# Half of the stored queries keep their centred products, and their features are made when attention takes them

## The chip, the cores and the metric

The kernel runs on one core of one Trainium2 chip. The metric is the device time of one execution in microseconds (us), here the median of several runs. All arithmetic is float32, and products are made from operands that are split into a high and a low part.

## The reference

The input `x` has 2048 rows of 512 columns. Every row is normalised, and the normalised rows go through two branches, whose results are multiplied.

```
xn  = layernorm(x)
q, k, v = split(xn @ wqkv)              # 32 heads of 16
phi(t) = where(t > 0, t + 1, exp(t)) + 1e-6
kv  = sum over rows of phi(k) v ;  z = sum over rows of phi(k)
s   = (phi(q) kv) / (phi(q) z + 1e-6) @ wo
h   = gelu(layernorm(xn) @ w1), its four column groups shifted by +1, -1, +2, -2 rows
x1  = xn + h @ w2
b   = x1 + gelu(layernorm(x1) @ w3) @ w4     # hidden width 1376
out = x + s * silu(b)
```

What matters here is `phi(q)`, the feature of a query. It is needed only after `kv` and `z` are complete, that is, after all rows have passed once. Since `where(t > 0, t + 1, exp(t))` equals `min(exp(t), 1) + relu(t)`, it also equals `exp(-relu(-t)) + relu(t)`.

## The kernel before, in words

The rows are worked on in 16 tiles of 128 rows; four tiles make a block (`QT` = 4, `NQ` = 4 blocks). The program has two stages.

In the first stage, up to about 235 us, every block passes through keys and queries, the sums over keys (`gram`) and the mixer (`mixer`, `mix2`, `mixed`). Blocks 0 and 1 make keys and queries by `key` and `query`, one tile at a time. Blocks 2 and 3 make them in `keys_queries` (line 839), a pair of tiles at a time with seven products in place of eight; its tiles `p1`, `p5` and `u2` hold products that are already centred. The key features are made there and then by `feature_k`: on ACT (ScalarE) a Relu into `kr` and an Exp into `kt`, then on DVE (VectorE) a scalar_tensor_tensor of the two. The query features are made by `feature_q` (line 802): on ACT a Relu of the negated product into `e`, a Relu into `r`, and an Exp of `e`; then `r` is stored in memory as `pqd` by SP's queue, and `e` is added to it there by a DMA that POOL (GpSimd) issues with accumulation (`gather`, line 220). In the profile these are the names `qe` and `qr`, and the transfers `pqd<-qr` and `pqd<-qe`. `by_chunk` and `by_block` are views that reorder the columns on the way.

In the second stage the four blocks go one after the other through the large products (`up_pair`, `down`), attention and the gate. Within a block, `turn_q` (line 1168) is called for two tiles when group 2 of the columns is worked on and for the other two at group 3. It fetches the stored features (`pq<-pqd`) and divides them by their denominators on DVE: a scalar_tensor_tensor into `qz`, a reduction into `den`, a reciprocal into `rd`, another scalar_tensor_tensor; then it turns them by way of memory. `forms_q` and `attend_pair` take what it leaves. ACT in this stage evicts the products (`p`, `u`, `p1s` and so on), makes the Gelus (`gf`, `f_..`) and the Tanhs of the gate (`th`). Exp and Gelu need different function tables on ACT; Relu, Copy and Identity run with either.

After each block's mixer, `mixed` (line 988) makes the second normalisation: statistics on DVE, then on POOL `w`, `rs` (a power) and `nm`, then on ACT the four tiles `y`, which DVE turns and SP stores.

The order of every engine's instructions is not the order of the calls. `Plan.emit` takes the operations as a graph, gives each a due time that is worked out back from a nominal sequence on TensorE, and lays them out one by one on the engines with estimated durations; among those ready it takes the one that is due first. So a change of one operation can reorder all the later ones on every engine. `SOONER` is a table of pairs, an operation's number in the graph and a number of quarter microseconds by which it is due earlier. Tiles named `p` come from 96 pieces of memory in SBUF, and `mm` and `acc` are the eight banks of PSUM.

Of the kernel before, what the change touches and what calls it, by code (L numbers as in the profile page):

```python
# [10 lines left out]
AF = mybir.ActivationFunctionType  # L11
ALU = mybir.AluOpType
# [384 lines left out]
def linear_attn_gated_by_mixer(  # L397
# [20 lines left out]
    QT = 4  # L418
# [7 lines left out]
    PIECE = BT + W  # L426
    EARLY = (), ()
    SUMS = "DVE"
    SOON = {"T": 30.0, "u": 5.0}
    AHEAD = 70.0, 50.0, 30.0, 10.0, 0.0  # L430
    TH = BT // 2
# [11 lines left out]
    pl = Plan(nc, pools, counts, ("acc", "mm"))  # L443

    def piece(name, dt=F32):
        return pl.new("p", name, dt, PIECE)[:, :512]

    def rounds(name):

        return piece(name + "h", F32R), piece(name + "l", F32R)  # L450

    def memory(name, width=512, rows=P):
        return pl.new("dram", name, F32, width, rows)
# [4 lines left out]
    def fixed(name, n, dt=F32):  # L458

        t = pl.new("const", name, dt, n)  # L460
        t.ap = const.tile([P, n], dt, name=name)
        return t
# [38 lines left out]
    rs1, rs2, ns1, nm1, nm2, au = (fixed(n, NT) for n in ("rs1", "rs2", "ns1", "nm1", "nm2", "au"))  # L501
# [31 lines left out]
    def col(t, i):  # L533
        return t[:, i:i + 1]
# [55 lines left out]
    def small(name, n):  # L590
        return pl.new("sm", name, F32, n)
# [80 lines left out]
    def make_u(b):  # L672
# [12 lines left out]
        for n, u, v, op in ((0, q[1, 0], q[1, 1], ALU.add), (1, parts[0], q[0, 0], ALU.subtract),  # L685
                            (2, q[0, 0], q[1, 0], ALU.subtract), (3, q[0, 1], parts[1], ALU.subtract)):
            for c in range(2):
                pl.tt(parts[n][c], u[c], v[c], op, eng=SUMS)
            hl = rounds(f"us{b}_{n}")
# [36 lines left out]
    def by_chunk(v):  # L726

        return v.via(lambda ap: ap.rearrange("p (c b k) -> p c b k", b=P // RB, k=RB))

    def by_block(v):  # L730

        return v.via(lambda ap: ap.rearrange("p (b c k) -> p c b k", b=P // RB, k=RB))
# [67 lines left out]
    pqd = {i: memory(f"pqd{i}") for i in range(NT)}  # L800

    def feature_q(i, t):
        e, r = (piece(f"q{n}{i}") for n in "er")
        pl.act(by_block(e), by_chunk(t), AF.Relu, scale=col(ns1, i))
        pl.act(by_block(r), by_chunk(t), AF.Relu, scale=col(rs1, i))
        pl.act(e, e, AF.Exp, scale=-1.0)
        pl.soon(pl.store(pqd[i].all, r))
        pl.soon(pl.gather(pqd[i].all, e))

    def query(i):  # L810
        ps = bank(f"q{i}")
        project(ps, i, WQ, range(NC))
        t = piece(f"qt{i}")
        pl.stt(t, qneg, mean(mv1, i), ps, ALU.mult, ALU.add)
        feature_q(i, t)
# [23 lines left out]
    def keys_queries(b, j):  # L839

        i, k = b * QT + j, b * QT + j + 2
        pa, pb, pe = (bank(f"{n}k{i}") for n in ("pa", "pb", "pe"))
        p1, p5, u2 = (piece(f"{n}k{i}") for n in ("p1", "p5", "u2"))

        def go(ps, x, y, start=True):
            products(ps, [both(U[b][x][c], j * P, (j + 1) * P) + TW[y][c] for c in range(2)], start, more=not start)

        go(pb, "a11", "b11")
        pl.act(p1, pb, AF.Copy)
        go(pe, "s1", "t1")  # L850
        pl.act(p5, pe, AF.Copy)
        go(pb, "s2", "t2", False)
        pl.act(u2, pb, AF.Copy)
        go(pa, "a12", "b21")
        pl.tt(p1, pa, p1, ALU.add)
        go(pb, "s3", "t3", False)
        pl.tt(p5, pb, p5, ALU.add)
        go(pe, "s4", "b22", False)
        pl.tt(u2, u2, pe, ALU.add)
        feature_k(i, p1, True)  # L860
        go(pb, "a22", "t4", False)
        feature_k(k, pb, True)
        feature_q(i, u2)
        feature_q(k, p5)
# [303 lines left out]
    def turn_q(i):  # L1168

        pq, t = piece(f"pq{i}"), piece(f"qz{i}")  # L1170
        pl.fetch(pq, pqd[i].all)
        pl.stt(t, pq, TINY, zb, ALU.add, ALU.mult)
        den, rd = small(f"den{i}", H).all, small(f"rd{i}", H).all
        pl.add("DVE", .6, .68, [t], [den], lambda: nc.vector.tensor_reduce(
            den.get(), t.get().rearrange("p (h d) -> p h d", d=DH), axis=AX.X, op=ALU.add))
        pl.ts(den, den, DEN_EPS, None, ALU.add)
        pl.add("DVE", .28, .35, [den], [rd], lambda: nc.vector.reciprocal(rd.get(), den.get()))
        v = pq.via(lambda ap: ap.rearrange("p (h d) -> p h d", d=DH))
        pl.stt(v, v, TINY, rd.via(lambda ap: ap[:, :, None].to_broadcast([P, H, DH])), ALU.add, ALU.mult)
        turned = Turned(f"q{i}", 1)  # L1180
        turned.put(0, pq)
        turned.take()
        QTT[i] = turned
# [208 lines left out]
    for what, *args in ORD:  # L1392
        pl.early = SOON.get(what, 0.0)
        DO[what](*args)
# [11 lines left out]
    for base, s in ((0, 1), (DH - 1, -1)):  # L1406
        v = bmask.all.via(lambda ap: ap.rearrange("p (h d) -> p h d", d=DH))
# [35 lines left out]
    for b in range(NQ):  # L1443
# [5 lines left out]
        for n, fs in enumerate(groups):  # L1449
# [14 lines left out]
            if n > 0:  # L1464
                for k in range(2):
                    if n == (2, 3)[k]:
                        for j in range(2):
                            turn_q(b * QT + 2 * k + j)
                        forms_q(b * QT + 2 * k)
                    if n == (4, 5)[k]:  # L1470
                        pairs.append(b * QT + 2 * k)
# [18 lines left out]
        else:  # L1490
# [3 lines left out]
            t = piece(f"xi{i}", F32R)  # L1494
# [13 lines left out]
                gate(b * QT + QT - 1, a, o, D // 2, late=True, by_dma=False, whole=o > 0)  # L1508

    SOONER = (  # L1510
        36, 64, 186, 8, 199, 16, 1412, -8, 1489, 8, 1493, 41, 1549, 16, 1982, 4, 2419, -8, 2854, 16, 3165, 8,
        4113, -8, 4394, -8, 4725, 64, 4805, 16, 4810, 65, 4814, -32,
    )
    pl.emit(first=6.0, lead={"p": 14.0, "w": 14.0, "ab": 10.0}, reserve={"p": 20, "w": 1, "ab": 0}, window=12.0,
            ahead=6.0, table=SOONER)
# [37 lines left out]
```

## Time and profile before

| | |
|---|---|
| median of 3 runs | 517.55 us |
| lowest and highest | 516.91 and 520.1 us |
| the profiled execution | 517.69 us, of it a span of 515.8 us from the first to the last instruction |
| granted TensorE clock | 0.999 |
| instructions in the span | 8950 |

The profile is of one execution. Its engines are PE (TensorE's products), PEld (its weight loads), DVE, ACT, POOL and SP. A row of a timeline gives the start and the duration in us, then the engine, the line, the operation, the tile written and the tiles read, the shape and the count, and in brackets the idle time of the engine before it with what ended it. Most rows name the line of a helper (L147 for products, L168 for ACT, L190, L195 and L200 for DVE and POOL, L224 for the DMAs that POOL issues), so the names of the tiles tell what is what. The end of a product is modelled: a product of 512 columns is shown with about 0.4 us, while the next one starts 0.23 us after it.

### The profile page before, as it was taken

What the parts mean: (1) busy time and instruction counts of PE and PEld (TensorE: products, weight loads), DVE (VectorE), ACT (ScalarE), POOL (GpSimd) and SP (SyncE); (2) the same over time, 40 slices, a digit from 0 to 9 for tenths busy, and PEclk for the clock granted to TensorE, in tenths of its full rate; (3) what the DMA queues carried; (4) which work ended last, traced back from release to release, by engine and by line L of the source; (5) the groups of instructions that cost most, each with busy time, mean ns of one, the idle gap of its engine ahead of it and who ended that gap; (6) DMA issues with size and microseconds to landing.
All of it is one profiled execution on the core that took longest, in us unless ns stands there. A gap on an engine that the chain in (4) does not pass through costs nothing.

```text
span 515.8 us, 8950 instructions
## 1 busy us (share of the span) xinstructions
PE 507.6 (98%) x2983; PEld 441.1 (86%) x2983; DVE 412.4 (80%) x832; ACT 337.9 (66%) x694; POOL 104.6 (20%) x191
## 2 busy tenths in 40 slices
PE   9999999999999999999999999999999999999996
PEld 7677788898778878898899989899898898999985
DVE  5987669999879996989999998655796659965545
ACT  5899778775979989878767644355443455643521
POOL 1589311244521732211100011000020000110000
PEclk9999999999999999999999999999999999999999
DMA  8978961989695999999875859577486594499404
GB/s 274 318 206 153 287 153 36 263 254 247 218 267 155 244 318 249 281 183 334 286 212 155 281 174 254 180 191 209 132 212 227 179 233 156 114 278 303 119 5 120
DMA packets 78194, 109.05 MB, mean 211 GB/s; under 512 B 8396, under 2 KB 31460, under 8 KB 78148
## 3 DMA queue, kind: packets, MB, share of 16 engines
q1 hardware_dynamic: 68788, 91.44, 55.5%
q0 software_dynamic: 9360, 17.04, 19.8%
q8 instruction: 23, 0.38, 0.3%
q14 instruction: 23, 0.19, 0.1%
HBM read 67.15 MB, written 32.91 MB: 194 GB/s over the span
## 4 chain that ended last, share of the span: by engine, by line
PE 77%; ACT 14%; DVE 3%; DMA 2%; issue 2%; POOL 1%; SPq 0%; ACTq 0%; DVEq 0%; POOLq 0%
PE acc L147 23%; PE pb L147 11%; PE pe L147 6%; PE pbs L147 4%; PE h L147 4%; PE g L147 4%; PE k L147 3%; PE pbm L147 3%; PE pa L147 3%; PE pes L147 2%; PE a L147 2%; ACT qe L168 2%; PE pbk L147 2%; PE q L147 2%; DMA o<-x 2%
## 5 line engine op out<-in xcount | busy, mean ns | idle before, releaser
L224 POOL DMA_DIRECT2D th<-in_x x14 | 12.4, 939 | 245.8 <-DVE th L200 108.5
L224 POOL DMA_DIRECT2D o<-x x16 | 14.6, 975 | 59.7 <-DVE o L190 47.3
L168 ACT ACTIVATE p<-pb 128x256 f32<-128x256 f32 x20 | 7.6, 382 | 27.3 <-PE pb L147 27.1
L190 DVE TENSOR_TENSOR gf<-pa,p 128x256 f32<-128x256 f32 x20 | 8.4, 418 | 18.8 <-PE pa L147 15.3
L168 ACT ACTIVATE th<-xo 128x512 f32<-128x512 f32 (+1 forms) x16 | 9.8, 620 | 20.0 <-DVE xo L190 19.9
L224 POOL DMA_DIRECT2D zacc<-kr x16 | 15.2, 949 | 36.8 <-DVE kr L200 22.7
L168 ACT ACTIVATE gf<-gf 128x512 f32<-128x512 f32 (+1 forms) x40 | 20.8, 523 | 0.8
L168 ACT ACTIVATE p<-pe 128x256 f32<-128x256 f32 x20 | 7.7, 384 | 17.5 <-PE pe L147 17.5
L224 POOL DMA_DIRECT2D pqd<-qe x16 | 14.8, 927 | 20.4 <-DMA pqd<-qr 8.8
L190 DVE TENSOR_TENSOR xo<-acc,xo 128x512 f32<-128x512 f32 (+1 forms) x16 | 10.4, 670 | 10.6 <-PE acc L147 9.6
L190 DVE TENSOR_TENSOR gf<-u,pe 128x256 f32<-128x256 f32 x20 | 8.3, 417 | 9.9 <-PE pe L147 9.8
L168 ACT ACTIVATE y<-o,nm,rs 128x512 f32<-128x512 f32 x16 | 12.1, 803 | 3.4 <-POOL nm L195 3.4
L168 ACT ACTIVATE ht<-ht 128x512 f32<-128x512 f32 x16 | 9.7, 626 | 6.5 <-DVE ht L190 6.4
L200 DVE SCALAR_TENSOR_TENSOR kr<-kt,kr 128x512 f32<-128x512 f32 x16 | 10.9, 683 | 3.7 <-ACT kt L168 3.6
L190 DVE TENSOR_TENSOR ht<-h,abc 128x512 f32<-128x512 f32 x16 | 10.7, 680 | 3.4 <-PE h L147 3.4
L168 ACT ACTIVATE x<-x,nm,rs 128x512 f32<-128x512 f32 x16 | 12.8, 810 | 0.0
L168 ACT ACTIVATE u<-pb 128x256 f32<-128x256 f32 x20 | 7.7, 384 | 6.0 <-PE pb L147 6.0
L200 DVE SCALAR_TENSOR_TENSOR th<-th,so 128x512 f32<-128x512 f32 (+1 forms) x17 | 10.9, 653 | 0.5
L200 DVE SCALAR_TENSOR_TENSOR pq<-pq,rd 128x512 f32<-128x512 f32 x16 | 11.0, 687 | 0.2
L601 POOL TENSOR_TENSOR rs<-w,nhalf 128x4 f32<-128x4 f32 (+2 forms) x10 | 10.7, 1074 | 0.7
L200 DVE SCALAR_TENSOR_TENSOR qz<-pq,zb 128x512 f32<-128x512 f32 x16 | 10.7, 685 | 0.2 <-DMA pq<-pqd 0.2
L168 ACT ACT_TABLE_LOAD x8 | 10.3, 1283 | 0.9 <-PEq L1544 0.8
(1682 smaller groups left out, 2239.1 us busy)
## 6 DMA issues: line engine op xcount, KB each, us to landing
w_s<-in_w SPq DMA_DIRECT2D x28, 256.0 KB, 4.7
x<-in_x SPq DMA_DIRECT2D x16, 256.0 KB, 3.5
zacc<-kr POOLq DMA_DIRECT2D x16, 256.0 KB, 5.1
pqd<-qr SPq DMA_DIRECT2D x16, 256.0 KB, 3.2
pqd<-qe POOLq DMA_DIRECT2D x16, 256.0 KB, 6.7
o<-x POOLq DMA_DIRECT2D x16, 256.0 KB, 6.3
x1d<-o SPq DMA_DIRECT2D x16, 256.0 KB, 5.7
pq<-pqd SPq DMA_DIRECT2D x16, 256.0 KB, 3.5
```

The source lines that it names most:

```text
L147: lambda: nc.tensor.matmul(out.get(), lhs.get(), rhs.get(), start=start, stop=stop, skip_group_check=more))
L168: nc.scalar.activation(out.get(), src.get(), func, scale=get(scale), **kw)
L190: self.vec(eng, out, [a, b], lambda: self.e(eng).tensor_tensor(out.get(), a.get(), b.get(), op=op), True)
L200: lambda: self.nc.vector.scalar_tensor_tensor(out.get(), a.get(), get(s), b.get(), op0=op0, op1=op1),
L224: lambda: self.nc.gpsimd.dma_start(out.get(), get(src), accum_op=ALU.add), mb=mb)
L601: lambda: g.tensor_tensor(out.get(), src.get(), nh.get(), op=ALU.pow))
```

## The change

For the tiles of the last two blocks (numbers 8 to 15), `feature_q` only stores the centred product. `turn_q` fetches it and makes the feature there, as keys have it: Relu, Exp, and min and sum in one scalar_tensor_tensor. The tiles of blocks 0 and 1 stay as they are. The table `SOONER` is another one: it has 13 pairs in place of 17. The graph has eight operations less.

```diff
+    LATE = 2 * QT
...
     def feature_q(i, t):
+        if i >= LATE:
+            pl.soon(pl.store(pqd[i].all, t))
+            return
         e, r = (piece(f"q{n}{i}") for n in "er")
         pl.act(by_block(e), by_chunk(t), AF.Relu, scale=col(ns1, i))
         pl.act(by_block(r), by_chunk(t), AF.Relu, scale=col(rs1, i))
         pl.act(e, e, AF.Exp, scale=-1.0)
...
     def turn_q(i):
         pq, t = piece(f"pq{i}"), piece(f"qz{i}")
-        pl.fetch(pq, pqd[i].all)
+        if i < LATE:
+            pl.fetch(pq, pqd[i].all)
+        else:
+            v, r = piece(f"qv{i}"), piece(f"qr{i}")
+            pl.fetch(v, pqd[i].all)
+            pl.act(by_block(r), by_chunk(v), AF.Relu, scale=col(rs1, i))
+            pl.act(by_block(pq), by_chunk(v), AF.Exp, scale=col(rs1, i))
+            pl.stt(pq, pq, 1.0, r, ALU.min, ALU.add)
         pl.stt(t, pq, TINY, zb, ALU.add, ALU.mult)
...
     SOONER = (
-        36, 64, 186, 8, 199, 16, 1412, -8, 1489, 8, 1493, 41, 1549, 16, 1982, 4, 2419, -8, 2854, 16, 3165, 8,
-        4113, -8, 4394, -8, 4725, 64, 4805, 16, 4810, 65, 4814, -32,
+        50, 32, 186, 2, 666, 16, 711, 8, 780, 4, 1431, 16, 2110, 16, 2323, 16, 3582, 16, 4095, 32, 4672, 32,
+        4788, 32, 4797, 16,
     )
```

## The prediction

> **What bounds the kernel now.** I read the page's parts 1 and 2 first, then busy time by stretches, then the timelines of the engines around each hole of PE.
>
> ```profile
> span 515.8 us, 8950 instructions
> PE 507.6 (98%) x2983; PEld 441.1 (86%) x2983; DVE 412.4 (80%) x832; ACT 337.9 (66%) x694; POOL 104.6 (20%) x191
> ```
>
> PE is busy for all but 8.2 us of the span. The number of products does not change, so a gain can only come out of those 8.2 us, while a loss can be of any size. Where they lie is seen in the stretches (columns: stretch, its length, then busy time and count of PE, PEld, DVE, ACT, POOL; granted clock; DMA share; GB/s):
>
> ```profile
> 0.00:20.00 20.00, 18.70 (x70) 13.94 (x71) 14.21 (x29) 12.90 (x26) 4.58 (x19) 1.00 0.89 314
> 20.00:60.00 40.00, 39.30 (x169) 30.42 (x168) 32.05 (x64) 37.90 (x69) 30.40 (x66) 1.00 0.88 208
> 60.00:120.00 60.00, 60.00 (x339) 52.01 (x338) 52.83 (x105) 45.02 (x86) 16.38 (x26) 1.00 0.74 192
> 120.00:220.00 100.00, 98.65 (x476) 80.41 (x474) 87.22 (x182) 86.78 (x157) 35.36 (x60) 1.00 0.92 246
> 140.00:160.00 20.00, 19.03 (x85) 14.73 (x84) 15.62 (x32) 16.57 (x31) 4.62 (x7) 1.00 0.84 236
> 220.00:240.00 20.00, 19.88 (x147) 17.64 (x146) 18.41 (x38) 14.61 (x37) 3.45 (x4) 1.00 0.98 241
> 240.00:500.00 260.00, 260.00 (x1728) 237.04 (x1727) 199.69 (x404) 138.63 (x319) 12.67 (x16) 1.00 0.68 200
> 360.00:480.00 120.00, 120.00 (x791) 109.19 (x790) 88.04 (x174) 58.25 (x134) 7.05 (x8) 1.00 0.69 201
> 500.00:520.00 20.00, 11.03 (x67) 9.61 (x65) 8.01 (x15) 2.07 (x4) 1.75 (x2) 0.92 0.30 79
> ```
>
> The idle time of PE is 1.30 us in the first 20, 0.70 at 20 to 60, nothing at 60 to 120, 1.35 at 120 to 220 (0.97 of it in the 20 us from 140 on), 0.12 at 220 to 240, nothing at 240 to 500, and 15.8 - 11.03 = 4.77 at the end; that adds up to 8.24. So the second stage, where the new work goes, has no hole today, and the first stage between 20 and 240 us, which loses work, has 2.17 us, nearly half of it at 140 to 160. That is the place to look at.
>
> ```profile
> 147.14 0.39 PE L147 MATMUL g<-k10h,x10l 128*128 128x512 f32 x1
> 148.01 0.50 PE L147 MATMUL pbk<-wk_0h,u_0h 128*128 128x512 f32 x1 [0.47 <-DVE ht L190]
> 148.34 0.39 PE L147 MATMUL pbk<-wk_0l,u_0h 128*128 128x512 f32 x1
> 148.57 0.40 PE L147 MATMUL pbk<-wk_0h,u_0l 128*128 128x512 f32 x1
> ...
> 150.66 0.40 PE L147 MATMUL pek<-kq_1h,us_0l 128*128 128x512 f32 x1
> 151.47 0.50 PE L147 MATMUL pbk<-kq_0h,us_1h 128*128 128x512 f32 x1 [0.41 <-ACT p1k L168]
> ...
> 154.84 0.40 PE L147 MATMUL pek<-wq_2h,us_3l 128*128 128x512 f32 x1
> 155.32 0.50 PE L147 MATMUL pbk<-kq_0h,us_2h 128*128 128x512 f32 x1
> ```
>
> A product's end is modelled, so I go by starts. From 148.34 to 148.57 the step is 0.23 us. The steps 147.14 to 148.01, 150.66 to 151.47 and 154.84 to 155.32 are 0.87, 0.81 and 0.48, so the holes are 0.64 + 0.58 + 0.25 = 1.47 us. The first waits for DVE, the second for ACT. What made them late stands some microseconds earlier:
>
> ```profile
> 138.84 0.36 DVE L596 BATCH_NORM_AGGREGATE mv<-st 128x2 f32<-128x6 f32 x4
> 140.47 0.94 POOL L224 DMA_DIRECT2D pqd<-qe  x1 [2.89 <-ACT qe L168]
> 141.48 0.33 POOL L195 TENSOR_SCALAR w<-mv 128x4 f32<-128x4 f32 x1
> 144.13 0.24 POOL L195 TENSOR_SCALAR nm<-nm 128x4 f32<-128x4 f32 x1
> 144.41 2.93 ACT L168 ACTIVATE y<-o,nm,rs 128x512 f32<-128x512 f32 x4 [3.40 <-POOL nm L195]
> 145.25 1.42 DVE L156 STREAM_TRANSPOSE y_0z<-y 128x512 f32<-128x512 f32 x2 [3.53 <-ACT y L168]
> 147.30 1.25 DVE L190 TENSOR_TENSOR ht<-h,abc 128x512 f32<-128x512 f32 x2
> 147.36 1.28 ACT L168 ACT_TABLE_LOAD   x1
> 150.85 0.57 ACT L168 ACTIVATE p1k<-pbk 128x512 f32<-128x512 f32 x1
> ```
>
> POOL works in order. Its accumulating transfer for a query waited 2.89 us for the Exp of `qe`, and behind it stood the second normalisation of block 1 (`w` to `nm`), whose statistics `mv` were there at 139.2. So ACT stood idle for 3.40 us before the four `y` and DVE for 3.53 before their transposes; then both had everything at once. DVE came to `ht` at 147.30, and PE's bank was freed late; ACT did the four `y`, a table load and Gelus before it evicted `p1k` at 150.85.
>
> **The change part by part.** The prices of the removed and the moved work:
>
> ```profile
> L168 ACT ACTIVATE qe<-qe x16: 613/619/642, 37.5 to 204.2; 128x512 f32<-128x512 f32 x16
> L168 ACT ACTIVATE qe<-p5k,ns x4: 710/722/729, 138.0 to 202.4; 128x512 f32<-128x512 f32 x4
> L224 POOL DMA_DIRECT2D pqd<-qe x16: 853/878/1218, 38.4 to 209.5; - x16
> L200 DVE SCALAR_TENSOR_TENSOR kr<-kt,kr x16: 657/684/693, 21.9 to 199.5; 128x512 f32<-128x512 f32 x16
> L168 ACT ACTIVATE kt<-p1k,rs x4: 709/717/724, 130.5 to 195.2; 128x512 f32<-128x512 f32 x4
> L168 ACT ACT_TABLE_LOAD x8 | 10.3, 1283 | 0.9 <-PEq L1544 0.8
> ```
>
> *Removed, eight times, at 128 to 210 us:* on ACT two Relus of 0.72 (that into `qr` has the shape of that into `qe`) and an Exp of 0.62, 2.06 us, together 16.5; on POOL one issue of 0.88, together 7.0; in memory one accumulating transfer of 256 KB, together 2.1 MB. ACT and DVE are the crowded engines there, yet what counts is PE's holes alone. With no query transfer in POOL's order, `w` can start when `mv` is there, at 139.2 in place of 141.48: 2.3 us earlier, as are the `y`, their transposes, the table load and the Gelus behind them. The three holes are 0.64 us and less, so 2.3 us closes all: **1.47 us**. The bounds are 0 (the new order has a wait of the same size in another place, since ACT, DVE and the key's own transfers stay crowded) and, for all idle time at 20 to 240 us, 2.17 plus the 1.47 - 0.97 = 0.50 that the modelled ends hide: 2.7. I take 1.47, for it is the only part whose cause the change removes.
>
> *The store* stays one issue of SP for a tile; it waits for DVE's product and no longer for a Relu of ACT, so it is not later. No table load goes away there: the keys' Exps stay, and with them the switches.
>
> *Added, eight times, at some 370 to 470 us:* on ACT a Relu and an Exp like those of the keys, 0.72 + 0.72, together 11.5; on DVE one more scalar_tensor_tensor of 0.68, together 5.5. Of both engines there is enough (ACT 58 and DVE 88 of 120 at 360 to 480). The Exps now stand among Gelus and Tanhs, so each pair of tiles costs a table load before and one behind: eight more, 10.3 us more of ACT. Over the span that makes ACT 337.9 - 16.5 + 11.5 + 10.3 = 343.2, DVE 412.4 + 5.5 = 417.9, POOL 104.6 - 7.0 = 97.6.
>
> Here is the risk. ACT works in order, and what stands behind a pair's Exps are the evictions (`p`, `u`, `f`) that PE's next products wait for. With the loads a pair holds ACT for 1.28 + 0.72 + 0.72 + 1.28 = 4.0 us at one piece.
>
> ```profile
> 371.25 1.27 ACT L168 ACTIVATE th<-xo 128x512 f32<-128x512 f32 x2 [4.00 <-DVE xo L190]
> 394.51 0.38 ACT L168 ACTIVATE p<-pb 128x256 f32<-128x256 f32 x1 [4.45 <-PE pb L147]
> ```
>
> ACT has free stretches of 4.00 and 4.45 us just ahead of and in block 2, so a pair fits, barely; and the order can put products into `acc`, which need no eviction, in front of an eviction that is late. Bounds: 0 for all four pairs, and 4 x 4.0 = 16 us if nothing covers them. I take 0, the nearer row being the free stretch of 4.45 us.
>
> The added Relu is also a new wait of ACT for a DMA. It is short of time only once:
>
> ```profile
> 386.82 0.87 SPq L218 DMA_DIRECT2D pq<-pqd  x2
> 390.70 1.29 DVE L200 SCALAR_TENSOR_TENSOR qz<-pq,zb 128x512 f32<-128x512 f32 x2
> ```
>
> There the fetches are issued 3.9 us before DVE uses them. With Relu, Exp and the new step in between the fetch must go about 3 us earlier on SP's queue, or `qz` comes 3 us later; the column group that uses the result is two groups on. I take 0; the bound is one tile's 1.4 us of ACT and 0.7 of DVE, once.
>
> *The table `SOONER`.* It moves due times also ahead of 120 us, where the work is the same. Its price shows in no row; the idle time of 0.70 us at 20 to 60 could go or double, so it lies within 0.7 us either way, and I take 0.
>
> [...] The rows of a load and of what follows show what a switch takes here:
>
> ```profile
> 205.84 1.28 ACT L168 ACT_TABLE_LOAD   x1
> 207.14 1.15 ACT L168 ACTIVATE ht<-ht 128x512 f32<-128x512 f32 x2
> ```
>
> The load takes 1.28 us, and the next instruction starts 0.02 us behind it. [...]
>
> *Sum.* The profiled execution took 517.69 us, 1.89 more than its span, and the median of the runs is 517.55, so the two are alike. 517.69 - 1.47 + 0 + 0 = **516.2 us**.
>
> **The rivals.**
>
> *The stall moves.* For it: ACT and DVE are busy 87 of 100 us at 120 to 220 by the stretches, the key's accumulating transfers stay in POOL's order, and every later instruction is laid out anew. Against it: the chain above runs through one query transfer. Then the time is that of before within the 0.7 us of the table, 517.7 (517.0 to 518.4). The same comes out if the removed transfers were hidden anyway.
>
> *Slower: Exps in the way of evictions.* Place: ACT at 370 to 470 us. Each pair that is not covered costs up to 4.0 us; it decides as soon as 1.5 us are uncovered. One pair uncovered and the gain gone: 517.7 + 4.0 = 521.7; all four, 533. For it: PE has no spare time there and a pair fits only just. Against it: ACT is idle for more than half of that stage. Chiefly I expect one pair: about 520 with the gain, 521.7 without.
>
> *A switch costs twice its row.* Then a pair holds ACT for 6.6 us, 2.1 over the longest free stretch above; four pairs make 8.4, and the time is 516.2 + 8.4 = 524.6. Against it stand the 0.02 us behind the load.
>
> *More than expected.* To come out over 1% lower (5.2 us, about what a measurement of this kernel can tell from no change) the 2.7 us of idle time at 20 to 240 would all have to go, the 1.3 at the start, and 1.2 of the tail's 4.77, which no part of the change touches but the table.
>
> **How the numbers follow.** Forecast 0.45, stall moves 0.33, Exps in the way 0.17, switch twice its row 0.02, more than expected 0.03. The low end is 517.69 less the 2.7 us of idle time, less the 0.6 by which the lowest run lies below the median, 514.3 with rounding. The high end is one uncovered pair without the gain, 521.7. Over 1% slower, above 522.7, needs two uncovered pairs or the dear switch: half of 0.17 and the 0.02, rounded to 0.10; over 1% faster 0.03; the rest 0.87.
>
> **What would show it.** Right: no query transfer in POOL's order; the `y` of block 1 without the wait of 3.4 us before them; no PE hole of 0.5 us or more at 140 to 160; 16 table loads; ACT near 343, DVE near 418, POOL near 98 us; PE at 20.00 in the stretches from 240 to 500. Wrong: PE waits for `p`, `u` or `f` after 360 us; more than 16 loads (the two Exps of a pair apart); the query's fetch as releaser of ACT; or new holes before 240 us as large as the old.

## The result, and the profile after

The changed kernel takes 518.89 us (median of 22 runs, 516.0 to 520.75); the kernel before, run beside it, 517.33 us (22 runs, 516.81 to 520.1). The ratio is 1.0026, interval 1.0013 to 1.0038: slower by 0.26%, some 1.3 us, where 1.47 us less was forecast. Both kernels scatter over 4 us, so each timing below is read with its interval and each reason by traces.

The profiled execution after took 518.31 us. Its totals, from the page's part 1 and one group of part 5:

```profile
span 516.6 us, 8955 instructions
PE 507.4 (98%) x2983; PEld 439.6 (85%) x2983; DVE 418.1 (81%) x840; ACT 343.9 (67%) x692; POOL 100.4 (19%) x183
L168 ACT ACT_TABLE_LOAD x14 | 18.0, 1283 | 3.9 <-PE pb L147 3.0
```

ACT's 343.9 us and DVE's 418.1 came out as counted (343.2 and 417.9). POOL's 100.4 us are 2.8 more than the 97.6 counted, about as much as a single instruction of POOL, `w`, will be seen to last too long. There are 14 table loads and not 16, since the four tiles of block 3 share one pair of loads.

To see where time went, the span is cut at three products: the first of block 0's mixer, the first of the second stage, and the last of all. From PE's timeline, before:

```profile
63.41 0.40 PE L147 MATMUL h<-u_0h,w_0h 128*128 128x512 f32 x1
...
234.44 0.68 PE L147 MATMUL a<-yb110h,w_lh 128*96 128x256 f32 x1
...
510.75 0.28 PE L147 MATMUL accx<-w_9h,f_9l 128*128 128x256 f32 x1
```

and after:

```profile
62.90 0.40 PE L147 MATMUL h<-u_0h,w_0h 128*128 128x512 f32 x1
...
234.57 0.28 PE L147 MATMUL a<-yb110h,w_lh 128*96 128x256 f32 x1
...
511.52 0.28 PE L147 MATMUL accx<-w_9h,f_9l 128*128 128x256 f32 x1
```

The differences of these starts, here and in each experiment's trace (us; "tail" is the rest of the span):

| kernel | span | start | middle | second stage | tail |
|---|---|---|---|---|---|
| before | 515.8 | 63.41 | 171.03 | 276.31 | 5.05 |
| after | 516.6 | 62.90 | 171.67 | 276.95 | 5.08 |
| b_look (before again) | 515.3 | 63.59 | 170.43 | 276.24 | 5.04 |
| a_look (after again) | 517.4 | 63.98 | 171.31 | 276.98 | 5.13 |
| a_again (after again) | 517.9 | 62.91 | 172.94 | 276.95 | 5.10 |
| a_evict_first | 517.4 | 62.82 | 172.49 | 277.02 | 5.07 |
| a_dve_waits | 515.8 | 63.12 | 170.60 | 277.03 | 5.05 |
| a_both | 516.3 | 63.69 | 170.56 | 276.96 | 5.09 |
| a_waits_all | 515.7 | 63.43 | 170.10 | 277.11 | 5.06 |
| b_waits_all | 518.0 | 65.70 | 170.37 | 276.82 | 5.11 |
| b_gather_behind | 515.0 | 63.94 | 169.75 | 276.22 | 5.09 |
| b_table_of_after | 521.7 | 63.37 | 177.08 | 276.22 | 5.03 |
| a_table_of_before | 518.4 | 65.81 | 168.87 | 278.53 | 5.19 |
| a_mixed | 515.3 | 63.45 | 168.65 | 278.03 | 5.17 |
| a_mixed_waits | 516.8 | 64.78 | 168.93 | 277.88 | 5.21 |
| a_exp_twice | 544.1 | 63.31 | 170.02 | 305.70 | 5.07 |
| a_no_loads | 516.7 | 63.38 | 171.66 | 276.63 | 5.03 |

After against before: start -0.5, middle +0.6, second stage +0.6. Some of this is the cut itself. In before the second stage's first product is shown with 0.68 us and the next one starts 0.52 us after it; in after it is 0.28 and 0.12. The 0.40 us between them belong to a product `m` right ahead, which thus counts in the second stage in the one case and in the middle in the other. (With 0.68: before, `b_look`, `b_waits_all`, `b_gather_behind`, `a_table_of_before`, `a_mixed`, `a_mixed_waits`; the others have 0.28.) With `m` counted alike, after's middle is 0.2 us longer than before's and its second stage 1.0. So the middle, which was to get 1.47 us shorter, got no shorter, and the second stage is not free. The start varies by itself: with the old table it is 63.4 to 63.9 us in three traces and 65.7 to 65.8 in two. Such a step of 2.2 us would make the two groups in which the runs of before fall (about 517.3 and 519.7); no run of before itself was traced in the upper one (where the start is lost, the last section says). The median of before lies between 517.3 and 518.8 from one set of runs to another, as fewer or more of its runs fall into that group, so a ratio is compared only with those of its own set.

The stretches of after, with the columns of those of before:

```profile
20.00:60.00 40.00, 39.66 (x171) 30.98 (x170) 32.39 (x65) 37.02 (x67) 28.52 (x66) 1.00 0.90 224
...
120.00:220.00 100.00, 97.48 (x471) 79.83 (x470) 87.86 (x182) 76.14 (x135) 31.40 (x51) 1.00 0.83 228
140.00:160.00 20.00, 20.00 (x103) 16.77 (x101) 17.41 (x35) 18.51 (x34) 2.02 (x4) 1.00 0.77 241
220.00:240.00 20.00, 20.00 (x153) 18.08 (x152) 18.00 (x37) 13.46 (x34) 3.42 (x4) 1.00 0.77 206
240.00:500.00 260.00, 259.75 (x1723) 235.30 (x1722) 203.89 (x408) 155.18 (x341) 13.18 (x16) 1.00 0.68 199
```

The 20 us from 140 on are full (before 19.03), yet the 100 us around them have 2.52 us of idle time (before 1.35). The stall was removed, and a larger one stands elsewhere. The removal, by POOL's and ACT's timelines of after:

```profile
137.52 0.57 POOL L195 TENSOR_SCALAR w<-mv 128x4 f32<-128x4 f32 x1 [0.77 <-DVE mv L597]
...
141.29 2.94 ACT L168 ACTIVATE y<-o,nm,rs 128x512 f32<-128x512 f32 x4 [2.53 <-POOL nm L195]
```

Block 1's `w` now waits for its statistics alone, 0.77 us, and the `y` start 3.1 us earlier (before 144.41), 2.6 counted from the mixer's first product. The new stall is in the same place of the next block, after's second normalisation of block 2 (POOL, then DVE, ACT and PE in the same stretch):

```profile
182.01 0.89 POOL L224 DMA_DIRECT2D zacc<-kr  x1 [7.67 <-DVE kr L200]
182.98 3.17 POOL L195 TENSOR_SCALAR w<-mv 128x4 f32<-128x4 f32 x1
...
182.89 0.69 DVE L200 SCALAR_TENSOR_TENSOR k12l<-kr,k12h 128x512 fp32r<-128x512 f32 x1
183.49 0.69 DVE L190 TENSOR_TENSOR x14l<-x,x14h 128x512 fp32r<-128x512 f32 x1
...
185.37 0.69 DVE L190 TENSOR_TENSOR w_al<-w_s,w_ah 128x512 fp32r<-128x512 f32 x1
185.98 0.69 DVE L200 SCALAR_TENSOR_TENSOR k14l<-kr,k14h 128x512 fp32r<-128x512 f32 x1
...
188.22 1.52 ACT L168 ACTIVATE y<-o,nm,rs 128x512 f32<-128x512 f32 x2 [2.27 <-POOL nm L195]
189.64 0.57 ACT L168 ACTIVATE p1k<-pbk 128x512 f32<-128x512 f32 x1
...
187.76 0.40 PE L147 MATMUL pek<-kq_1h,us_0l 128*128 128x512 f32 x1
190.27 0.50 PE L147 MATMUL pbk<-kq_0h,us_1h 128*128 128x512 f32 x1 [2.11 <-ACT p1k L168]
```

Read it from below. PE steps 2.51 us where 0.23 is usual, a hole of 2.28, because ACT evicts `p1k` behind two `y`, and the `y` come late. POOL's `w` is why: four numbers a row, 0.57 us in block 1, and here 3.17. All that time DVE runs one instruction after another, six of them, and `w` ends at 186.15, right behind the sixth, `w_al` (186.06); the seventh, `k14l`, runs on beside its end. That DVE is the cause is so far an argument.

### The profile page after: what moved, and what is told of

Same layout as the page of the kernel before. It is cut to its first block, busy times and chain, and to the rows that moved or that the text cites. A ratio compares the mean times of both kernels' runs of the same rounds, so it can differ in the third digit from the quotient of the medians.

```text
span 516.6 us, 8955 instructions
## 1 busy us (share of the span) xinstructions
PE 507.4 (98%) x2983; PEld 439.6 (85%) x2983; DVE 418.1 (81%) x840; ACT 343.9 (67%) x692; POOL 100.4 (19%) x183
## 4 chain that ended last, share of the span: by engine, by line
PE 82%; ACT 7%; DVE 5%; DMA 3%; issue 2%; POOL 1%; SPq 1%; DVEq 0%; POOLq 0%
PE acc L147 21%; PE pb L147 10%; PE h L147 9%; PE g L147 5%; PE pe L147 5%; PE pbs L147 4%; PE pbm L147 4%; PE pbk L147 3%; PE pa L147 2%; PE pes L147 2%; PE a L147 2%; PE pem L147 2%; PE k L147 2%; PE q L147 2%; DMA o<-x 1%
## 5 line engine op out<-in xcount | busy, mean ns | idle before, releaser
L596 DVE BATCH_NORM_STATS2 st<-o 128x6 f32<-128x512 f32 x16 | 10.4, 683 | 1.0 <-DMA o<-x 1.0
L190 DVE TENSOR_TENSOR so<-so,xo 128x512 f32<-128x512 f32 (+1 forms) x16 | 10.7, 669 | 0.1
```

The lines of the kernel that those rows point to most:

```text
L190: self.vec(eng, out, [a, b], lambda: self.e(eng).tensor_tensor(out.get(), a.get(), b.get(), op=op), True)
L596: pl.add("DVE", .62, .69, [xv], [st], lambda: nc.vector.bn_stats(st.get(), xv.get()))
```

## The experiments

Labels beginning with a are edits of the kernel after, with b of the kernel before. Diffs are cut to their core; numbers are operations of the graph.

**The new stall.** Three runs ask whether ACT's order or POOL's `w` makes it.

`a_evict_first` lets `p1k` go ahead of the `y`:

```diff
+    hold (y8, y9 and the first transpose of y8) until eviction p1k of tile 13's pair is issued
```

> The kernel after with one move: on ACT the eviction p1k of block 3's first pair stands ahead of the first two y of block 2's second normalisation, not behind them; every other order is the same. Theory 1 (the loss is the one hole of 2.3 us at 188 us, where PE waits for p1k behind two late y): the hole goes, 2.0 to 2.3 us less than after, 516.6 to 516.9, faster than before by 0.5 us or so. Rival (the loss lies in the second stage, in Exps and table loads): no change, 518.9. Rival (the table of due times as such): a hole of like size opens some us later, 518 to 519.

Measured: 518.96 us (12 runs) against 518.84 of before, ratio 1.001 (0.9995 to 1.0025). The hole moves to the next eviction; POOL, then PE, of this kernel:

```profile
182.68 3.17 POOL L196 TENSOR_SCALAR w<-mv 128x4 f32<-128x4 f32 x1
...
192.38 0.51 PE L148 MATMUL pbk<-kq_0h,us_2h 128*128 128x512 f32 x1 [1.74 <-ACT u2k L169]
```

So ACT's order only chooses which eviction is late; `w` is as long as before.

`a_dve_waits` makes DVE wait for POOL's results in block 2, with two copies of 128x4:

```diff
         pl.ts(w, var(mv2, a, z), EPS, None, ALU.add, eng="POOL")
+        if b == 2: nc.vector.tensor_copy(gap, w)     # issued right behind w
         power(r, w, QT)
+        if b == 2: nc.vector.tensor_copy(gap, r)     # issued right behind rs
```

> The kernel after with two tiny DVE copies of 128x4 that read the results w and rs of block 2's second normalisation, so that DVE stands still until POOL has made them. Theory 1a (w lasts 3.17 us in place of 0.3 because DVE's back-to-back instructions with two SBUF inputs keep POOL from its operands): w takes 0.3 to 0.6 us and rs 1.1, the y start 1.5 to 2.2 us earlier, the hole at 188 falls from 2.3 us to under 0.8, 517.0 to 517.6. Rival 1b (w is slow of itself, behind the transfer that POOL has just issued): w still lasts 3 us, DVE stands for 3 us too, the hole stays or grows, 519 to 521.

Measured: 517.4 us (12 runs), ratio 0.998 (0.9962 to 0.9998). POOL, DVE, ACT and PE:

```profile
183.70 0.70 POOL L196 TENSOR_SCALAR w<-mv 128x4 f32<-128x4 f32 x1
...
184.43 0.17 DVE L1015 COPY gap<-w 128x4 f32<-128x4 f32 x1
...
187.40 1.51 ACT L169 ACTIVATE y<-o,nm,rs 128x512 f32<-128x512 f32 x2
...
189.44 0.50 PE L148 MATMUL pbk<-kq_0h,us_1h 128*128 128x512 f32 x1 [0.57 <-ACT p1k L169]
```

The same `w` takes 0.70 us, ACT no longer idles before the `y`, and the wait at `p1k` falls from 2.11 to 0.57, while one at `p5k` ahead of it grows from 0.41 to 0.98. In the same set of runs the unaltered changed kernel (`a_again`, next) took 519.34 us, so the copies take 1.9 us off it. That two small copies which add work to the busier engine win time shows that the new stall was POOL held up by DVE. In both traces `w` ends 0.09 us behind a DVE instruction: here behind `k12l` (183.62 to 184.31), the one that ran when `w` started, and in after behind the sixth in a row, after 3.17 us. Which property of these instructions holds POOL up is not shown.

`a_again` is the changed kernel unaltered, in the same set of runs.

> The kernel after once more, for its spread (516.0 to 520.75 us) against that of before. Theory 1a: its length varies with the hole at 188 us, whose size depends on when POOL gets between DVE's instructions; a profile at another total time shows another duration of w and another hole, and nothing else of size. Rival (the second stage): w and the hole are as in the first profile, 3.2 and 2.3 us, and the difference lies after 360 us.

Measured: 519.34 us (12 runs), ratio 1.0007 (0.9989 to 1.0026). Before beside it has a median of 518.84 here, so this set does not show the loss of the first comparison beyond its interval: the loss is small, and its size is uncertain. In the trace `w` takes 3.17 us and the hole is there, but the middle is 1.3 us longer than in the first trace of after. PE's timeline, and its stretch of 5 us:

```profile
190.12 0.72 PE L147 MATMUL pbk<-kq_0h,us_1h 128*128 128x512 f32 x1 [2.10 <-ACT p1k L168]
190.63 0.63 PE L147 MATMUL pbk<-kq_0l,us_1h 128*128 128x512 f32 x1
191.06 0.63 PE L147 MATMUL pbk<-kq_0h,us_1l 128*128 128x512 f32 x1
...
193.62 0.41 PE L147 MATMUL pak<-wk_2h,u_2l 128*128 128x512 f32 x1
193.87 0.39 PE L147 MATMUL pak<-wk_3h,u_3h 128*128 128x512 f32 x1
...
190.00:195.00 5.00, 4.88 (x14) 3.88 (x15) 4.38 (x10) 3.59 (x7) 0.00 (x0) 0.66 1.05 307
```

Behind the hole products step by 0.43 us, and from 193.6 on by 0.25: the granted clock is 0.66 of full there. The last section has more on it.

`a_look` and `b_look` are one run each of both kernels, unaltered, on a second chip.

> The kernel after, a third look. Theory 1a: one of two pictures: w of block 2 lasts 3.17 us, a hole at p1k of about 2.1 us and a time of 518.3 or more; or w lasts 0.7 us, a hole below 0.6 and a time below 517.7. Rival: w and the time do not go together.

> The kernel before, a second look. If its time is near 517.3, the holes of the first profile; if it is near 519.5, one more hole of 2 us or a stretch of lower clock, and the profile shows which.

Measured: 519.05 and 517.22 us. `w` takes 3.18 us and PE waits 2.09 in `a_look`; `b_look` has the holes of before. So all three traces of after have the stall, and both traces of before are without it.

`a_both` joins the copies with an order in which `p1k` goes ahead of the first two `y`, and DVE's `p5k` ahead of one weight split and one statistic.

> The kernel after with the DVE waits for w and rs, the eviction p1k ahead of the first two y, and on DVE the sum p5k of block 3's first chain ahead of one split and one statistic. Theory 1: the first alone left holes of 1.0 (p5k) and 0.6 us (p1k) at 180 to 190 us; with the moves both fall to 0.3 or less, so about 1.2 us less than with the waits alone, 516.0 to 516.4, and faster than before by 1 us or more. Rival (ACT is full there, one eviction put ahead makes the next one late, as when p1k was moved alone): the holes come back at p5k or u2k of block 3, 517.4.

Measured: 517.88 us (12 runs), ratio 0.9986 (0.9969 to 1.0003). The middle is 170.56, that of the copies alone is 170.60: the waits at `p5k` and `p1k` are gone, and one of 0.81 us at `u2k` and one of 0.40 at `k12h` stand in their place. The 516.0 to 516.4 expected did not come: moving single instructions by hand only moved the wait.

`a_waits_all` has the copies in all four blocks; `b_waits_all` has them in the kernel before, with the query transfer of the next paragraph moved too.

> The kernel after with the two DVE copies behind w and rs in all four blocks' second normalisations, not in block 2's alone. Theory 1a (a race for the operands between POOL's w and DVE's row of instructions, mostly lost in block 2, is what the time of after varies by): the runs lie close together, none of the group at 518.3 to 520 that makes up most of after's; median 517.0 to 517.6, and no w over 1 us. If the other blocks have no such race, no gain over the waits in block 2 alone (517.4). Rival (the spread comes from the clock or the start): two groups 2 us apart as in after.

> The kernel before with the same copies in all four blocks, and the first query transfer of block 2 behind block 1's normalisation. On two of three chips before has a second group of runs 2 us above the first (517.4 and 519.7). If that is the same race in one of its blocks: one group, 516.2 to 516.9. Rival (its second group has another cause, the start or the clock): two groups, 516.7 and 519.1, as with the transfer moved alone.

Measured: `a_waits_all` 517.46 us (12 runs), ratio 0.9993 (0.9979 to 1.0007), middle 170.10, so no lower time than with the copies in block 2 alone; and `b_waits_all` 519.26 us (12 runs), 1.0022 (1.0002 to 1.0042), slower than before, start 65.70. Its runs still fall in two groups, 517.8 to 518.7 and 519.9 to 521.4, so this race is not what parts the runs of before.

**The old stall.** `b_gather_behind` leaves the kernel before as it is, but issues the query transfer `pqd<-qe` of tile 10 behind block 1's `nm` on POOL.

```diff
+    hold (pqd<-qe of tile 10) until nm of block 1 is issued
```

> The kernel before with one move: the first query transfer of block 2 on POOL (pqd<-qe of tile 10) is issued behind block 1's second normalisation and not ahead of it. If the prediction's chain holds (w waits behind that transfer, so the y, the transposes and the evictions are late): the 3.4 us of idle time ahead of the y shrink to 1.5 or less, the holes at 147 to 155 us (1.47 us) go, 515.9 to 516.3. Rival (DVE and ACT are too full there anyway, or POOL's small operations are held up by DVE in the same way): the holes stay, 517.3.

Measured: 518.36 us (12 runs), ratio 0.9997 (0.9978 to 1.0017), which decides nothing: these runs too lie in two groups. The trace says more; ACT, then PE:

```profile
143.26 2.94 ACT L169 ACTIVATE y<-o,nm,rs 128x512 f32<-128x512 f32 x4 [2.27 <-POOL nm L196]
...
154.54 0.50 PE L148 MATMUL pbk<-kq_0h,us_2h 128*128 128x512 f32 x1 [0.45 <-ACT u2k L169]
```

The `y` start 1.15 us earlier, though the wait ahead of them shrinks only to 2.27 us and not to 1.5. Two of the three holes are gone, and one wait of 0.45 us is left. The middle is 169.75 us against 171.03 and 170.43: 0.7 to 1.3 us less. The chain that the prediction drew was real, and by these traces moving one transfer was worth half of its 1.47 us or more.

**Graph or table.** `b_table_of_after` is the graph of before with the new `SOONER`, numbers shifted to the same operations; `a_table_of_before` is the changed graph with the old one.

> The kernel before with the new table of due times alone, its numbers carried over to the same operations. Theory 1 (the loss is an accident of one order: POOL's w among DVE's back-to-back instructions, and an eviction behind y): this order has holes of its own, not those of after; in its profile w of block 2 lasts under 1 us; 517 to 519, with holes between 20 and 240 us of 1 to 3 us in all. Rival (the table is what costs): the same hole at p1k of block 3 as after, 518.9. Rival (features alone): as before, 517.3, with the holes of before.

> The kernel after with the old table of due times, carried over to the same operations. Theory 1: again another order; holes at 20 to 240 us of 0.5 to 3 us that depend on where w stands among DVE's instructions, none to speak of after 240; 516 to 519. Rival (late features cost by themselves): 518.9 or more, with PE idle after 360 us.

Measured: `b_table_of_after` 522.39 us (6 runs), ratio 1.0076 (1.0056 to 1.0095); and `a_table_of_before` 518.79 us (12 runs), 1.0006 (0.9989 to 1.0023). The first is above all that was expected. In `b_table_of_after` the middle is 177.08 us, 6 more than before, with a new hole and a lower clock behind it (PE, and its stretch):

```profile
160.04 0.56 PE L147 MATMUL pbm<-w_b11h,ha112h 128*128 128x256 f32 x1 [2.35 <-ACT ha112h L168]
...
120.00:180.00 60.00, 56.89 (x278) 46.80 (x277) 52.45 (x112) 50.43 (x88) 23.66 (x41) 0.97 0.74 204
```

In `a_table_of_before` the middle is 168.87, 1.6 to 2.2 less than before, but the start is the long one and the second stage 278.53, with waits for the Gelus in it, so PE does stand idle after 360 us, as the rival had it:

```profile
PE pe L147 <- ACT gf L168: 0.6, 1, 0.6
...
PE pb L147 <- DVE gf L190: 0.3, 1, 0.3
```

So neither the removed work alone nor the table alone sets the time: the middle ranges over 8 us by the order.

`a_mixed` joins them: the new table's entries for the start, the old one's from 1404 to 1950, the new one's for the second stage. `a_mixed_waits` adds the copies of block 2.

```diff
     SOONER = (
-        50, 32, 186, 2, 666, 16, 711, 8, 780, 4, 1431, 16, 2110, 16, 2323, 16, 3582, 16, 4095, 32, 4672, 32,
-        4788, 32, 4797, 16,
+        50, 32, 186, 2, 666, 16, 711, 8, 780, 4, 1404, -8, 1473, 8, 1477, 41, 1533, 16, 1950, 4,
+        2323, 16, 3582, 16, 4095, 32, 4672, 32, 4788, 32, 4797, 16,
     )
```

> The kernel after with a table of due times put together: the new one's entries ahead of 1400 and behind 2300, the old one's (carried over) between. Measured apart, the new table's start comes to the mixer's first product at 62.9 to 64.0 us, the old table's middle in the changed graph took 168.9 us from there to the second stage (before 170.4 to 171.0, after 171.3 to 172.9), and the new table's end took 277.0 (before 276.2). If the pieces keep those times in one order: 63.4 + 168.9 + 277.0 + 5.1 = 514.4 of span, 516.2 us, faster than before by 1 us. Rival (an order made anew has holes of its own wherever the pieces meet): 517 to 520.

> The same with the two DVE copies behind w and rs of block 2. If the pieces keep their times and w loses no race there: as the mixed table alone, 516.2 to 516.6. If the mixed order does lose the race for the operands: 2 us less than it, and no w over 1 us.

Measured: `a_mixed` 516.96 us (12 runs, 515.9 to 517.51), before beside it 517.72 (29 runs), ratio 0.9972 (0.9957 to 0.9986): faster than before in its set, by 0.3%. With the copies 517.35 us, 0.9985 (0.997 to 1.0001), no better. `a_mixed` by POOL, by stretches, and by PE in the second stage:

```profile
184.88 0.56 POOL L195 TENSOR_SCALAR w<-mv 128x4 f32<-128x4 f32 x1 [1.54 <-DVE mv L597]
...
120.00:180.00 60.00, 60.00 (x302) 49.81 (x302) 55.98 (x120) 45.95 (x82) 23.89 (x43) 1.00 0.78 222
180.00:240.00 60.00, 59.97 (x338) 50.79 (x337) 52.75 (x105) 44.96 (x91) 9.16 (x12) 1.00 0.91 247
...
422.87 0.38 PE L147 MATMUL pb<-yt32h,w_s1h 128*128 128x256 f32 x1 [0.70 <-ACT u L168]
```

`w` takes 0.56 us with no copies, PE is full from 120 to 240, and the middle is 168.65, 1.8 to 2.4 us less than before. The second stage did not keep the 277.0 that was expected: it gives 1.7 back, half of it (0.86 by starts) in the hole shown. The traced span is that of `b_look`; the median gains also because all its runs lie within 1.6 us, while 9 of the 29 of before lie above 518.8. That may be luck: `a_mixed_waits`, with the same entries for the start, has runs up to 519.7.

**The late features.** `a_exp_twice` makes them dearer: behind each late Exp a Gelu of 4 columns, then the Exp again, two more loads each time.

```diff
             pl.act(by_block(pq), by_chunk(v), AF.Exp, scale=col(rs1, i))
+            nc.scalar.activation(gap, nhalf, AF.Gelu_apprx_tanh)                     # issued right behind
+            nc.scalar.activation(by_block(pq), by_chunk(v), AF.Exp, scale=col(rs1, i))
```

> The kernel after in the same order, with each late Exp followed by a Gelu of 4 columns and the same Exp once more: for each of the eight tiles two table loads and about 0.9 us more of ACT, 3.5 us, 28 us in all. If the second stage has room as the profile of after says (a pair holds ACT for 4 us in stretches where PE does not need it): twice the load for a pair is 11 us of ACT at one piece, more than any free stretch, and PE gets holes of 3 us or more at each of the four places, 525 to 540. If ACT's order there had slack of 10 us: no change, 518.9. Either way it shows how near the late Exps stand to the edge.

Measured: 547.48 us (6 runs), ratio 1.0557 (1.0526 to 1.0588), above the 525 to 540 expected. POOL, and PE's waits from 360 us on:

```profile
183.84 0.69 POOL L196 TENSOR_SCALAR w<-mv 128x4 f32<-128x4 f32 x1
...
PE pb L148 <- ACT p L169: 15.8, 3, 6.8
PE pe L148 <- ACT p L169: 7.2, 1, 7.2
```

An added Gelu and Exp take 1.28 + 0.20 + 1.28 + 0.72 = 3.5 us of ACT, 28 us for eight. PE waits four times for `p`, 23.0 us together, so the four places had some 5 us to spare between them (28 less 23, an estimate). The second stage is 28.7 us longer than in after, since the granted clock, 0.89 to 0.94 in the stretches from 360 us on, adds to the waits. The late Exps of after thus stand a little short of the point where more work costs its full length. By the way, `w` takes 0.69 us here although DVE runs the same order around it, and the middle is 170.02 us, 1.65 less than in after: the race can be won without any copy, and winning it is worth at least as much as the copies are.

`a_no_loads` leaves the late Exps out and makes Relus in their place, which needs no other table; six loads go.

> The kernel after in the same order with the eight late Exps made as Relus, so that the six table loads of the second stage fall away and the features of those tiles are other numbers. If the loads are what the second stage lost: from its first product to its last 276.2 to 276.4 us as before, in place of 277.0. If Relus, Exps and sums cost by themselves: 276.8 to 277.0. The first stage has the same order as after, so the time is 518.3 less what the second stage gives, or 2 us lower still where w wins the race.

Measured: 518.3 us (10 runs), ratio 1.0004 (0.999 to 1.0019); 8 loads in all, second stage 276.63 us, with the loads 276.95 to 277.03. The late features can be told from the rest by a cut at block 2, the first that has them; its first product in before, after and `a_no_loads`, and a row of after in block 0:

```profile
372.35 0.28 PE L147 MATMUL a<-yb112h,w_lh 128*96 128x256 f32 x1
372.54 0.28 PE L147 MATMUL a<-yb112h,w_lh 128*96 128x256 f32 x1
373.11 0.28 PE L147 MATMUL a<-yb112h,w_lh 128*96 128x256 f32 x1
...
258.37 0.39 PE L147 MATMUL pb<-yt20h,w_s0h 128*128 128x256 f32 x1 [0.23 <-ACT p L168]
```

From block 2's first product to the last of all it is 138.40 us in before, 138.98 in after and 138.56 without the loads. So the late features cost 0.6 us in after's order, and the loads are 0.4 of it. The other 0.2 us are spread over short steps of PE, no one row carries them, and that they belong to the functions and sums is not shown. The rest of what after's second stage lost is a hole of 0.4 us in block 0 (PE's step to this last row is 0.51 in place of 0.12), over 100 us ahead of the first late feature. `a_no_loads` has it too, so neither the loads nor the features make it.

## Why the prediction was wrong, step by step

*The chain at 140 to 160 us* was right: no query transfer before `w`, `y` of block 1 earlier by 3.1 us, or 2.6 from the mixer's first product (2.3 was said), no hole left there, and `b_gather_behind` shows the cause in the kernel before. That the wait of 3.4 us before the `y` would vanish was too much; 2.53 is left.

*"Closes all: 1.47 us"* is the step that failed. The size is right for the mechanism: the middle of `a_table_of_before` and `a_mixed`, where nothing new comes up, is 1.6 to 2.4 us shorter than before. But in the order that the new table gives, block 2's normalisation makes a hole of 2.28 us, more than the three that went, and in `a_again` the granted clock behind it is 0.66 of full over 5 us. The lower bound of the gain was set to 0 ("a wait of the same size in another place"); it had to go below, since nothing kept the new wait to the size of the old. `a_dve_waits` gives 1.1 us of the middle back against after, 0.7 against `a_look` and 2.3 against `a_again`. The prediction looked for what stood in POOL's queue ahead of `w` and not for what DVE does while `w` runs, though `w` to `nm` took 2.89 us in the quoted rows (141.48 to 144.37). That 518.89 us lies inside the stated range is luck: its upper end was the price of an uncovered pair of Exps, not of this hole.

*`SOONER` at 0 within 0.7 us* was mis-sized. Its bound came from the idle time at 20 to 60 us alone. On the old graph the new table costs 6 us in the middle; on the changed graph it costs 2.8 there against the old table (171.67 to 168.87) and saves 1.6 in the second stage, 0.4 of each being the product `m`. The table and the graph have one price together, and none apart.

*The late Exps at 0* was mis-sized too: from block 2 on 0.6 us in after's order. With the old table's middle the second stage is 1.7 (`a_mixed`) and 2.2 us (`a_table_of_before`) longer than before, 0.86 of the 1.7 in one hole for `u`; how much of that the late Exps are and how much the order is, no run parts. The rival "Exps in the way of evictions" had its place right; its price per pair did not come in after's order. `a_exp_twice` shows how little room was left.

*A switch costs twice its row* fell. ACT's timeline of after, in the second stage:

```profile
382.29 1.28 ACT L168 ACT_TABLE_LOAD   x1
383.58 1.34 ACT L168 ACTIVATE pq<-qv,rs 128x512 f32<-128x512 f32 x2
```

The Exps start 0.01 us behind a load of 1.28, and no run shows a switch of twice that row.

*The fetches* cost nothing that shows: no wait of PE or of ACT in the second stage names them. Of the rivals, "the stall moves" was nearest, but as a stall that grows.

## What to carry to other kernels

Where an engine is already full for 98%, removing a known stall is worth what the next order makes of it: bound the gain below zero by the longest wait that a moved instruction could newly cause, and treat an ordering table as fitted to one graph. Look for short POOL instructions on the way to a critical eviction, and at what DVE runs beside them; a `w` of 3.17 us for four numbers a row, in place of 0.57, is a sign of it. Of several runs of one kernel that scatter, take a trace of more than one before a reason is believed.

## What the runs showed of the hardware

*POOL can lose to six DVE instructions in a row.* The same 128x4 instruction took 3.17 or 3.18 us in five traces of after's order (after, `a_again`, `a_look`, `a_evict_first`, `a_no_loads`) and 0.69 in a sixth (`a_exp_twice`), with the same DVE instructions around it and the same start, 0.08 or 0.09 us behind that of `k12l`. It ends 0.08 or 0.09 us behind `w_al`, the sixth of them, in the five, and 0.09 behind `k12l`, the first, in `a_exp_twice`. What decides is not in the trace. It would explain after's three fastest runs (516.0 to 517.2 of 22), which were not traced.

*TensorE's clock fell behind three of the holes.* Behind holes of 2.1 us (`a_again`), 1.7 (`a_evict_first`) and 2.35 (`b_table_of_after`) stretches of 5, 10 and 60 us show a granted clock of 0.66, 0.83 and 0.97 of full. Each time that is 1.7 or 1.8 us of clock lost, as half rate for some 3.5 us gives (5 x 0.34, 10 x 0.17 and 60 x 0.03; an estimate); in `a_again` the steps of 0.43 us lasted 3.5 us, and the middle is 1.3 us longer than in the first trace of after. Behind equal holes of 2.1 us in after, `a_look` and `a_no_loads` the clock stayed at 1.00. So the length of the hole alone does not decide it, and what does is not in the traces.

*The start is longest where TensorE's first products take longest.* It takes 62.8 to 64.8 us in fifteen traces and 65.7 to 65.8 in two. The first products of PE, in before and in `b_waits_all`:

```profile
5.06 2.56 PE L147 MATMUL k<-wk_s,xt 128*128 128x512 f32 x4 [0.23 <-DMA xt<-in_xt]
...
5.85 3.75 PE L148 MATMUL k<-wk_s,xt 128*128 128x512 f32 x4 [1.02 <-DMA xt<-in_xt]
```

These four take 3.75 us in the two traces with the longest start and in the third, `a_mixed_waits` (64.78), and 1.95 to 3.02 in the other fourteen. In the three the product behind them takes 1.41 or 1.42 us, elsewhere 0.78 to 0.80, so it took some 1.8 times as long there, though the granted clock shows 1.00. Of the 2.3 us between the starts of before and `b_waits_all`, 1.3 are these slower products and 0.8 the later `xt`. What decides is not in the traces. The table does not: `a_mixed_waits` has the new one's entries for the start.
